# Attention and MoE on one core: batch 0 multiplies each score group with v at once, zero-padded shared block, half of batch 1 in split fp16

## The chip, the cores and the metric

One NeuronCore of a Trainium2 chip runs the kernel. The metric is the device time of one execution in microseconds (us), as the median of several executions. Each program runs alone on its core; there is no communication. TensorE (PE) multiplies into PSUM, ScalarE (ACT) and VectorE (DVE) work on the results, and SyncE (SP) issues nearly all transfers, in the order of its own instruction stream.

## The reference, cut to what matters

```python
# q, k, v: [4 batches, 12 heads, 448, 64] float32; cap = 30
scores = (q @ k.T) / sqrt(64)
scores = cap * tanh(scores / cap)
attn = softmax(scores, axis=-1)            # exp, row sum + 1e-9, division
x = (attn @ v) -> reshaped to [1792 tokens, 768]
h = x @ w_in                               # w_in [768, 2048]
g = h / (1 + exp(-1.702 * h))
out = g @ w_out                            # w_out [2048, 768]
# w_in and w_out arrive as float64, read as pairs of 32-bit words
```

## The kernel before, in words

**Units.** The attention is cut into 24 units (`units`): 4 batches of 6 head pairs. Everything is kept transposed, with keys or features on partitions and the 448 queries of a batch along the free dimension. The 448 keys of each of the two heads make three blocks of 128, and a last block of 64; the two last blocks share one tile of 128 partitions (block number 3, head j in half j). A unit has four score groups (`GROUPS`, line 482): blocks 0 and 4, 1 and 5, 2 and 6, then 3 alone. `scores` (484) multiplies a group into a PSUM tile `s`, takes tanh on ACT (tile `t`) and exp on ACT (tile `p`). The row sums `sm` come from a product with ones, the unnormalised result `pa` from a product with v (`attend`, 566, and `col_tiled`, 536).

**Two precisions.** Batches 0 and 1 (`F32_BATCHES = 2`) use float32 matmuls. Batches 2 and 3 split q, k, p and v into a high and a low fp16 part and add products; that needs casts and subtractions on ACT and DVE for each unit. For those batches the exp tiles of a unit are first added up on DVE (`addup`, tile `ta`).

**Shared block.** For block 3 the kernel uses half-height matmuls on the two halves (`COLS`, row slices), in the array tilings 64x64 and 64x32, while the other blocks use 128x64 and 128x32.

**Normalising.** Most units send their sums (`s4`, a copy of `sm` in ring `f`) to DRAM, fetch them spread over 112 partitions (`sd`, `sr`), invert them there, write them back (`rd`) and read them broadcast (`rb`): a trip of four steps of transfers through the one SP queue. The tile `pa` is copied to `pu` so that PSUM comes free. `DIRECT0` names two units of batch 0 whose sums are made at full width and inverted in place. The result goes to `xh` and `xl`, the fp16 parts of x.

**MoE.** Once the x of a batch is ready, `h_unit` (640) makes 16 feature chunks of 18 matmuls each, and `o_unit` (656) 6 output chunks of 48, all in split fp16; tile names `m`, `gh`, `gl`. `decode_w` (408) turns one fetched tile of weights into two fp16 parts with six operations; there are 24 tiles of w_in and 32 of w_out, and they are fetched by `fetch_w` into buffers which lie in the later w_out space, or in the ring `stg`.

**Order.** The main loop at line 742 calls everything in a program order: after each score group a `slot` adds weight decodes (`DECODE0`, `DECODE1`) and, against a time budget, MoE work. Delay lists (`AV_DELAY`, `SUM_DELAY0`, ...) put the steps of `attend` some slots later. Then `Plan.schedule` (199) simulates engines with the rates in `RATE` and lets the first operation that can start go first, by program order on a tie; it fixes the order on each engine and the buffer of each ring that an operation gets. A ring hands out its buffers in program order of the requests: the request at the head must be served first (line 212). Which engine runs a cast is fixed by `CAST_ON_ACT`, `G_ON_ACT`, `HI_ON_ACT`. On the chip, each engine follows that order and waits on semaphores.

**Start.** The value `cap` is fetched by a GpSimd DMA (line 315); its reciprocal, scaled, is the scale of the first tanh. Sixteen small matmuls on zeros run meanwhile.

Of the kernel before, what the change touches and what calls it, by code (L numbers as in the profile page):

```python
# [30 lines left out]
CAST_ON_ACT = ((), (0, 1), (0, 1, 2, 3), (0, 1, 2, 3))  # L31
G_ON_ACT, HI_ON_ACT = 18, 12
# [10 lines left out]
DMA_ISSUE, DMA_LAG, DMA_BW = 0.38, 2.1, 0.36  # L43
# [44 lines left out]
class Op:  # L88
    __slots__ = ("n", "eng", "us", "emit", "bufs", "left", "users", "ready", "turn", "mb", "start", "end", "tag", "prio")


class Plan:
    def __init__(self, tc):
        self.tc, self.nc = tc, tc.nc
        self.ops = []
        self.rings = []
        self.shift = 0
        self.after = []
# [5 lines left out]
    def ring(self, tiles):  # L104
        r = {"tiles": tiles, "free": [(0.0, i) for i in range(len(tiles))], "queue": []}
        self.rings.append(r)
        return r
# [7 lines left out]
    def op(self, eng, us, emit, writes, reads, turn=None, mb=0.0, tag=""):  # L115
        o = Op()
        o.n, o.eng, o.us, o.emit, o.turn, o.mb, o.tag = len(self.ops), eng, us, emit, turn, mb, tag
        o.prio = o.n + self.shift
# [24 lines left out]

    def act(self, out, in_, func, scale=1.0, bias=0.0):
        n = math.prod(out.shape[1:])
        kind = ("act", "act_ptr", "act_ptr2")[isinstance(scale, Ref) + isinstance(bias, Ref)]
        def emit():
            nc = self.nc
            if func == AF.Copy:
                nc.scalar.activation(real(out), real(in_), func, scale=scale, bias=bias)  # L150
            elif isinstance(bias, Ref):
                nc.scalar.activation(real(out), real(in_), func, scale=real(scale), bias=real(bias))  # L152
            else:
                nc.scalar.activation(real(out), real(in_), func, scale=real(scale))  # L154
        self.op("ACT", RATE[kind][0] + n * RATE[kind][1], emit, [out], [in_, scale, bias])

    def dve(self, name, out, ins, kind="dve", n=None, accum_out=None, **kw):

        f = RATE[kind]
# [5 lines left out]
        self.op("DVE", f[0] + n * f[1] + (0.08 if accum_out is not None else 0.0), emit, w, list(ins.values()))  # L165
# [7 lines left out]
    def scaled(self, out, in_, f):  # L173
        def emit():
            self.nc.vector.tensor_scalar_mul(real(out), real(in_), f)
        n = math.prod(out.shape[1:])
        self.op("DVE", RATE["dve2"][0] + n * RATE["dve2"][1], emit, [out], [in_])

    def copy(self, out, in_):
        def emit():  # L180
            self.nc.vector.tensor_copy(real(out), real(in_))
        n = math.prod(out.shape[1:])
        self.op("DVE", RATE["dve2"][0] + n * RATE["dve2"][1], emit, [out], [in_])

    def mm(self, us, turn, parts):
# [4 lines left out]
        self.op("PE", us, emit, [p[0] for p in parts], [y for p in parts for y in p[1:3]], turn=turn)  # L190

    def dma(self, pairs, mb):
# [3 lines left out]
        self.op("SP", DMA_ISSUE * len(pairs), emit, [p[0] for p in pairs], [p[1] for p in pairs], mb=mb)  # L196


    def schedule(self):
        free = {"PE": 0.0, "ACT": 0.0, "DVE": 0.0, "SP": 0.0}  # L200
        cand = {e: [o for o in self.ops if o.eng == e and not o.left] for e in free}
        turn, pipe = None, 0.0
        order = []
        while len(order) < len(self.ops):
            best = None
            for e, c in cand.items():
                for o in c:
                    t = max(o.ready, free[e])
# [4 lines left out]
                    if t < math.inf:  # L213
                        o.start = t
                        k = (max(t, free[e]), o.prio)
                        if best is None or k < best[0]:
                            best = (k, e, o)
                    else:
                        o.start = t
            assert best is not None, "no step can go on"  # L220
            (t, _), e, _ = best
            o = min((o for o in cand[e] if o.start <= t), key=lambda o: o.prio)
            cand[e].remove(o)
            for b in o.bufs:
                if b.slot is None:
                    b.ring["queue"].pop(0)
                    b.slot = b.ring["free"].pop(0)[1]
            us = o.us
            if e == "PE":
                us += PE_TURN * (o.turn != turn)  # L230
                turn = o.turn
            free[e] = t + us
# [6 lines left out]
            o.start, o.end = t, t + us  # L239
            order.append(o)  # L240
            for u in o.users:
                u.left -= 1
                u.ready = max(u.ready, t + us if u.eng == e and e != "SP" else done + HANDOFF)
                if not u.left:
                    cand[u.eng].append(u)
# [7 lines left out]
        return order  # L253
# [18 lines left out]
def fast_path(ctx, tc, flag, q, k, qx, kx, v, cap, w_in, w_out, out):  # L272
# [9 lines left out]
    NC = 7  # L282
# [21 lines left out]
    ones16 = sb.tile([P, 32], F16, name="ones16")  # L304
    nc.vector.memset(ones16, 1.0)
    ones32 = sb.tile([P, D], F32, name="ones32")
    nc.vector.memset(ones32, 1.0)
# [4 lines left out]
    for _ in range(16):  # L312
        nc.tensor.matmul(ps_m["tiles"][0][:32, :128], ones16, wz, start=True, stop=True)
    capt = sb.tile([P, 1], F32, name="capt")
    nc.gpsimd.dma_start(capt, cap.to_broadcast([P, 1]))
    lnb = sb.tile([P, 1], F32, name="lnb")
    nc.vector.memset(lnb, math.log(64.0))
# [7 lines left out]
    capt, lnb, ones16, ones32 = (plan.fixed(t) for t in (capt, lnb, ones16, ones32))  # L325
# [27 lines left out]
    NW, NA = 2 * W0 * 2, 2 * S  # L353
    early_w = plan.ring([t[:, i * NW:(i + 1) * NW].bitcast(I32).rearrange("p (n t) -> p n t", t=2) for i in range(3) for t in wo_t])
    early = [t[:, 10 * DM + i * NA:10 * DM + (i + 1) * NA].bitcast(F32) for i in range(5) for t in wo_t]
    early_kq = plan.ring(early[:6])
    early_v = plan.ring([t.rearrange("p (c d) -> p c d", d=D) for t in early[6:9]])
# [50 lines left out]
    def decode_w():  # L408
# [16 lines left out]
        if m == 0 and z < G_ON_ACT:  # L425
            plan.scaled(Hf, Hf, 2.0**-112)
        else:
            plan.act(Hf, Hf, AF.Copy, scale=2.0**-112)
        plan.stt(L, H, 3, L, ALU.logical_shift_left, ALU.bitwise_or)
        if m == 1:  # L430
            plan.after = early_bufs["w"] if r < 8 else early_bufs["a"] if r >= 10 else []
        if m == 0 and z < HI_ON_ACT:
            plan.scaled(hi, Lf, WS)
        else:
            plan.act(hi, Lf, AF.Copy, scale=WS)
# [8 lines left out]
    def load_qk(b, p, split):  # L444
# [10 lines left out]
        plan.act(kk, kd, AF.Copy, scale=QS)  # L455
# [4 lines left out]
        plan.act(qh, qd, AF.Copy, scale=QS)  # L460
# [23 lines left out]
    def scores(kt, qt, split, pt, act_cast, addup):  # L484
        qsplit = len(qt) == 2
        for g, cols in enumerate(GROUPS):
# [24 lines left out]
            if split:  # L511
# [6 lines left out]
                if g in act_cast:  # L518
                    plan.act(pb[:, 0, :nn], t[:, :nn], AF.Copy)
                else:  # L520
                    plan.copy(pb[:, 0, :nn], t[:, :nn])
# [12 lines left out]
            yield  # L534

    def col_tiled(o, pt, weights, prods, us):

        for i in range(4):
            parts = []
            for w, (a, bb) in enumerate(prods):  # L540
                for j in range(2):
                    c, rs = COLS[j][i]
                    lhs = ones32[rs] if weights is None else weights[a][rs, c]
                    parts.append((o[j * D:(j + 1) * D, :S], lhs, pt[c][bb][rs], i == 0 and w == 0, i == 3 and w == len(prods) - 1))
            plan.mm(us * len(prods), "64x64" if i == 3 else "128x64", parts)

    def attend_direct(pt, vt, xh, xl):
        sm, pa = plan.turn(ps_sm), plan.turn(ps_pa)
        col_tiled(sm, pt, None, [(0, 0)], 4 * FULL)
        s4 = plan.turn(f_r)  # L550
        plan.act(s4, sm[:, :S], AF.Copy, bias=1e-9)
        col_tiled(pa, pt, vt, [(0, 0)], 4 * FULL)

        def invert():
            plan.dve("tensor_reduce", new_rmin(), dict(in_=s4), n=S, op=ALU.min, axis=AX.X)

        def final():
            r = plan.turn(f_r)
            plan.dve("reciprocal", r, dict(in_=s4), kind="recip")
            plan.tt(r, pa[:, :S], r, ALU.mult)  # L560
            plan.act(xh, r, AF.Copy, scale=XS * VS)
            plan.stt(xl, r, XS * VS, xh, ALU.mult, ALU.subtract)

        return invert, final

    def attend(pt, vt, split, xh, xl, direct=False):
        if direct:
# [408 lines left out]
```

## Time and profile before

| | us |
|---|---|
| median of 3 runs | 661.16 (660.21 to 661.57) |
| the profiled execution's own time | 663.54 |
| span of the profiled execution | 661.4 |
| PE busy in the span | 638.3 (97%) |
| ACT busy | 389.2 (59%) |
| DVE busy | 371.8 (56%) |

A row of a busy table gives the share of the span, but the stages differ: the slices and the windows show them. An interval on a line of the timeline is start, then duration; a bracket behind it is how long the engine had been idle and what it waited for. "x8" counts instructions merged on the line; a float32 matmul appears as two. The unit 0 of the text is the first head pair of batch 0, and unit 6 the first of batch 1.

### The profile page before, as it was taken

Reading aid. Unit: us, or ns where it says so; the run is one execution under the profiler, and the core shown is the slowest. Engines: PE = TensorE matmul, PEld = TensorE weight load, DVE = VectorE, ACT = ScalarE, POOL = GpSimd, SP = SyncE. Lnnn points to the kernel's source line nnn. Section 1 sums busy time; section 2 is a strip of 40 time slices with the busy share of each in tenths; the row PEclk is TensorE's granted clock in tenths of the full one; section 3 lists DMA queues with packets and bytes.
Section 4 is the critical chain, followed back from the end, with each engine's and each line's share of the span. In section 5 each row is a group of like instructions: output and inputs, shape, how many; then the busy total and the mean of one; then the engine's idle time right before and its main releaser. Section 6 shows DMA issues by size and latency. Waiting matters only on the chain.

```text
span 661.4 us, 9003 instructions
## 1 busy us (share of the span) xinstructions
PE 638.3 (97%) x3474; PEld 288.5 (44%) x3474; DVE 371.8 (56%) x746; ACT 389.2 (59%) x557; POOL 0.9 (0%) x5
## 2 busy tenths in 40 slices
PE   6977999999999999999999999999999999999996
PEld 2222224433434445444444544544444455555553
DVE  4998898777765125767864545676764213332000
ACT  4866986878776546867975666787866203331000
POOL 0000000000000000000000000000000000000000
PEclk9988999999999999999999999999999999999999
DMA  8975512555556223022123322110010110000000
GB/s 288 381 270 140 171 46 57 141 152 162 152 174 201 80 62 98 15 85 71 29 71 99 91 65 85 50 49 16 16 42 16 30 42 14 1 1 15 15 29 31
DMA packets 38465, 58.70 MB, mean 89 GB/s; under 512 B 16056, under 2 KB 28176, under 8 KB 38416
## 3 DMA queue, kind: packets, MB, share of 16 engines
q1 hardware_dynamic: 38384, 58.06, 28.7%
q8 instruction: 29, 0.48, 0.3%
q14 instruction: 20, 0.16, 0.1%
q0 software_dynamic: 32, 0.00, 0.0%
HBM read 52.35 MB, written 5.70 MB: 88 GB/s over the span
## 4 chain that ended last, share of the span: by engine, by line
PE 89%; DMA 4%; ACT 3%; DVE 2%; issue 1%; SPq 0%; ACTq 0%; DVEq 0%; POOLq 0%
PE m L189 65%; PE s L189 10%; PE pa L189 9%; PE sm L189 4%; DMA sr<-sd 1%; ACT t L154 1%; DMA capt<-in_cap_dram 1%; ACT p L152 1%; DMA f<-rd 1%; DVE wo_l L163 1%; DVE wi_l L163 0%; DVE wo_h L163 0%; DMA rd<-rr 0%; DMA sd<-f 0%; SPq L195 0%
## 5 line engine op out<-in xcount | busy, mean ns | idle before, releaser
L189 PE MATMUL m<-xh,wi_h 128*128 128x448 f16 x384 | 135.8, 354 | 0.0
L189 PE MATMUL m<-xl,wi_h 128*128 128x448 f16 x384 | 135.6, 353 | 0.0
L189 PE MATMUL m<-xh,wi_l 128*128 128x448 f16 x384 | 135.6, 353 | 0.0
L189 PE MATMUL m<-gh,wo_h 128*128 128x448 f16 x384 | 135.5, 353 | 0.0
L189 PE MATMUL m<-gh,wo_l 128*128 128x448 f16 x384 | 135.4, 352 | 0.0
L189 PE MATMUL m<-gl,wo_h 128*128 128x448 f16 x384 | 135.3, 352 | 0.0
L154 ACT ACTIVATE t<-s,tsc 128x896 f32<-128x896 f32 x96 | 87.0, 909 | 39.1 <-PE s L189 38.9
L189 PEld LDWEIGHTS <-wi_h 128*128 128x128 f16 x768 | 73.3, 98 | 79.5 <-issue 12.5
L189 PEld LDWEIGHTS <-wo_h 128*128 128x128 f16 x768 | 73.7, 98 | 76.1 <-issue 9.2
L154 ACT ACTIVATE f<-m 128x448 f32<-128x448 f32 x64 | 34.8, 544 | 63.0 <-PE m L189 62.6
L163 DVE SCALAR_TENSOR_TENSOR f<-f,m 128x448 f32<-128x448 f32 x64 | 39.6, 619 | 49.3 <-ACT f L154 49.0
L150 ACT ACTIVATE f<-m 128x448 f32<-128x448 f32 x24 | 13.0, 540 | 87.1 <-PE m L189 79.0
L163 DVE TENSOR_TENSOR ta<-ta,t 128x896 f32<-128x896 f32 (+1 forms) x48 | 41.1, 856 | 31.0 <-ACT t L152 30.7
L189 PE MATMUL s<-qh,kk 128*128 128x448 f16 (+2 forms) x192 | 54.0, 469 | 1.4 <-ACT t L154 1.4
L163 DVE SCALAR_TENSOR_TENSOR gl<-f,gh 128x448 f16<-128x448 f32 x64 | 39.8, 622 | 26.6 <-ACT gh L150 26.5
L152 ACT ACTIVATE p<-t,lnb,capt 128x896 f32<-128x896 f32 (+1 forms) x48 | 49.4, 1038 | 7.1 <-PE pa L189 6.0
L189 PEld LDWEIGHTS <-wi_l 128*128 128x128 f16 x384 | 37.6, 98 | 35.2 <-issue 0.2
L189 PEld LDWEIGHTS <-wo_l 128*128 128x128 f16 x384 | 37.6, 98 | 35.1
L150 ACT ACTIVATE gh<-f 128x448 f16<-128x448 f32 x64 | 36.4, 568 | 14.0 <-DVE f L163 14.0
L189 PE MATMUL s<-wo_l,wo_h 64*128 64x448 f32 (+1 forms) x96 | 28.6, 694 | 11.4 <-ACT t L154 10.0
L163 DVE SCALAR_TENSOR_TENSOR stg<-stg 128x384 int32<-128x384 int32 x64 | 35.0, 558 | 4.2 <-ACT stg L150 3.2
L152 ACT ACTIVATE t<-t,lnb,capt 128x896 f32<-128x896 f32 (+1 forms) x36 | 36.2, 1007 | 1.0
(93 smaller groups left out, 625.0 us busy)
## 6 DMA issues: line engine op xcount, KB each, us to landing
stg<-in_moe_w_out_dram SPq DMA_DIRECT2D x32, 384.0 KB
wo_h<-in_moe_w_in_dram SPq DMA_DIRECT2D x12, 512.0 KB
wo_l<-in_moe_w_in_dram SPq DMA_DIRECT2D x12, 512.0 KB
out_dram<-f SPq DMA_DIRECT2D x24, 224.0 KB
stg<-in_kx_dram SPq DMA_DIRECT2D x12, 448.0 KB
stg<-in_qx_dram SPq DMA_DIRECT2D x12, 448.0 KB
f<-rd SPq DMA_DIRECT2D x44, 112.0 KB
vd<-in_v_dram SPq DMA_DIRECT2D x12, 224.0 KB
```

Of the source, the lines that this page charges most:

```text
L150: nc.scalar.activation(real(out), real(in_), func, scale=scale, bias=bias)
L152: nc.scalar.activation(real(out), real(in_), func, scale=real(scale), bias=real(bias))
L154: nc.scalar.activation(real(out), real(in_), func, scale=real(scale))
L163: getattr(self.nc.vector, name)(out=real(out), **{k: real(x) for k, x in ins.items()}, **kw, **a)
L189: self.nc.tensor.matmul(real(o), real(w), real(x), start=a, stop=z)
```

## The change

The change touches the order in which batch 0 is worked, the layout of the shared block, the start, and the planner.

- **v at once.** For float32 units, `attend_step` follows each score group with its share of `pa`, and with `sm` after groups 1 and 3 (each group for direct units). `sm` and `pa` are claimed at a unit's first group.
- **Zero padding.** v has 8 blocks: block 3 is stored twice, with the other head's half zeroed; `ones32` and `ones16` have three versions likewise. All of `pa` runs in tiling 128x64 and all of `sm` in 128x32 (128x64 for direct units).
- **Start.** `cap` is the first DMA of SP; an activation on a small tile (`warm`) loads the table of ACT early.
- **Split.** `F32_UNITS = 9`: units 9 to 11, the second half of batch 1, go in split fp16, with their row sums by four fp16 steps (no `addup`).
- **Planner.** Casts and PSUM copies may go to ACT or DVE, chosen in the simulation (`ways`, with `DVE_SHY`); the delay lists are gone; the ring `f` of six becomes `f` (3, any order), `rb` (2) and `pu` (2); the ring `p` goes from 6 to 5; `DMA_ISSUE` and `DMA_LAG` grow. Fewer weight tiles are decoded before batch 1 (`PAUSE`), more within it (`DECODE1`).

```diff
-DECODE1 = (1, 2)
-PAUSE = (2, 3)
-AV_DELAY = (0, 1, 2)
-SUM_DELAY0 = (1, 1, 2, 2, 3, 4)
-SUM_DELAY = (1, 2, 3, 3, 4, 5)
-DIRECT_DELAY = (5, 0)
-F32_BATCHES = 2
+DECODE1 = (2, 2)
+PAUSE = (2, 1)
+F32_UNITS = 9
-CAST_ON_ACT = ((), (0, 1), (0, 1, 2, 3), (0, 1, 2, 3))
-G_ON_ACT, HI_ON_ACT = 18, 12
+PE_STAY = 0
-DMA_ISSUE, DMA_LAG, DMA_BW = 0.38, 2.1, 0.36
+DMA_ISSUE, DMA_LAG, DMA_BW = 0.5, 2.6, 0.36
+ACT_FROM = 4.0
+DVE_SHY = 2.0
...
+    def scaled(self, out, in_, f=None, on="AV", psum=False, bias=None):
...
+        ways = {}
+        if "V" in on:
+            ways["DVE"] = (self.cost("dve" if psum else "dve2", n), on_dve)
+        if "A" in on:
+            ways["ACT"] = (self.cost("act", n), on_act)
+        self.op(ways, [out], [in_])
...
-                            t = max(t, r["free"][0][0]) if r["queue"][0] is b and r["free"] else math.inf
+                            t = max(t, r["free"][0][0]) if r["free"] and (r["any"] or r["queue"][0] is b) else math.inf
+                    p = o.prio + (PE_STAY if e == "PE" and o.turn != turn else 0)
+                    k = (t, p, o.ways[e][0])
...
-    NC = 7
+    NC = 8
...
+    capt = sb.tile([P, 1], F32, name="capt")
+    nc.sync.dma_start(capt, cap.to_broadcast([P, 1]))
+    lnb = sb.tile([P, 1], F32, name="lnb")
+    nc.vector.memset(lnb, math.log(64.0))
+
+    warm = sb.tile([P, 1], F32, name="warm")
+    nc.scalar.activation(warm, lnb, AF.Tanh)
+
+    ones32 = [sb.tile([P, D], F32, name=f"ones32_{i}") for i in range(3)]
+    ones16 = [sb.tile([P, 32], F16, name=f"ones16_{i}") for i in range(3)]
...
-    capt = sb.tile([P, 1], F32, name="capt")
-    nc.gpsimd.dma_start(capt, cap.to_broadcast([P, 1]))
...
-    p_t = [sb.tile([P, 2, 2, S], F16, name=f"p{i}") for i in range(6)]
+    p_t = [sb.tile([P, 2, 2, S], F16, name=f"p{i}") for i in range(5)]
-    f_r = ring([P, S], F32, "f", 6)
+    f_r = ring([P, S], F32, "f", 3)
+    f_r["any"] = True
+    rb_r = ring([P, S], F32, "rb", 2)
+    pu_r = ring([P, S], F32, "pu", 2)
...
-    COLS = (
-        [(0, slice(0, P)), (1, slice(0, P)), (2, slice(0, P)), (3, slice(0, D))],
-        [(4, slice(0, P)), (5, slice(0, P)), (6, slice(0, P)), (3, slice(D, P))],
-    )
+    COLS = (((0, 0), (1, 1), (2, 2), (3, 3)), ((4, 4), (5, 5), (6, 6), (3, 7)))
...
+    def row_sums(sm, pt, split, steps):
+        for i in steps:
+            parts = []
+            for w in range(2):
+                for j in range(2):
+                    k = i if split else 2 * i + w
+                    c, g = COLS[j][k][0], 2 * j + w
+                    one = 2 if k < 3 else j
+                    lhs, rhs = (ones16[one], pt[c][w]) if split else (ones32[one][:, :32], pt[c][0])
+                    parts.append((sm[32 * g:32 * g + 32, :S], lhs, rhs, i == 0, i == (3 if split else 1)))
+            plan.mm(FULL if split else 4 * FULL, "128x32", parts)
+
+    def attend_step(pt, vt, g, direct):
+        if g == 0:
+            pt["sm"], pt["pa"] = plan.turn(ps_sm), plan.turn(ps_pa)
+        if direct:
+            col_tiled(pt["sm"], pt, None, [(0, 0)], 4 * FULL, [g])
+        elif g % 2:
+            row_sums(pt["sm"], pt, False, [g // 2])
+        col_tiled(pt["pa"], pt, vt, [(0, 0)], 4 * FULL, [g])
...
-        split = b >= F32_BATCHES
+        split = u >= F32_UNITS
+        direct = b == 0 and p in DIRECT0
         tb = BUDGET[b]
-        for c, _ in enumerate(scores(kt, qt, split, pt, CAST_ON_ACT[b], split)):
-            if c == 1 and b:
+        x = xs[b, p] = [plan.turn(r) for r in x_r[p]]
+        for g in scores(kt, qt, split, pt, b >= 2):
+            if not split:
+                attend_step(pt, vt, g, direct)
+            if g == 1 and b:
                 prepare(u + 1)
-            slot(tb, DECODE1[p // 3] if b else DECODE0[c])
+            slot(tb, DECODE1[p // 3] if b else DECODE0[g])
...
+    last = _np.zeros((B, NP, 2, 128, D), vv.dtype)
+    last[:, :, 0, :64], last[:, :, 1, 64:] = vv[:, :, 0, 384:], vv[:, :, 1, 384:]
```

## Rows read from the trace of the kernel before

**Rows 1.** Windows: length, busy us and (count) of PE, PEld, DVE, ACT, POOL; granted clock, DMA share, GB/s.

```profile
10.00:40.00 30.00, 27.54 (x116) 6.49 (x116) 28.53 (x54) 25.31 (x28) 0.00 (x0) 1.00 1.02 383
40.00:94.00 54.00, 45.50 (x210) 13.14 (x209) 48.25 (x88) 42.05 (x60) 0.00 (x0) 0.94 0.50 142
94.00:120.00 26.00, 26.00 (x134) 11.58 (x134) 22.61 (x53) 15.73 (x29) 0.00 (x0) 1.00 0.21 61
120.00:200.00 80.00, 80.00 (x409) 32.21 (x406) 60.63 (x166) 64.26 (x107) 0.00 (x0) 1.00 0.55 154
200.00:260.00 60.00, 60.00 (x314) 25.83 (x313) 23.46 (x40) 35.63 (x48) 0.00 (x0) 1.00 0.34 105
```

**Rows 2.** Timeline, the first 10 us: cap, the first scores, the first tanh.

```profile
1.20 0.42 SPq L195 DMA_DIRECT2D wo_l<-in_q_dram  x1
1.24 0.66 POOL L315 DMA_DIRECT2D capt<-in_cap_dram  x1 [0.79 <-POOLq L950]
4.19 3.36 PE L189 MATMUL s<-wo_l,wo_h 64*128 64x448 f32 x8 [1.22 <-DMA wo_l<-in_q_dram]
...
8.14 0.16 DVE L319 RECIPROCAL rc<-capt 128x1 f32<-128x1 f32 x1 [7.00 <-DMA capt<-in_cap_dram]
...
9.87 1.01 ACT L154 ACTIVATE t<-s,tsc 128x896 f32<-128x896 f32 x1
```

**Rows 3.** Timeline, 27 to 78 us: sums, their copies, the transfers of units 0 and 2.

```profile
27.87 0.64 SPq L195 DMA_DIRECT2D sd<-f  x1
...
30.85 1.82 PE L189 MATMUL sm<-p,ones 128*32 128x448 f32 x8
...
44.38 0.53 ACT L150 ACTIVATE f<-sm 128x448 f32<-128x448 f32 x1
45.82 3.22 PE L189 MATMUL sm<-p,ones 128*32 128x448 f32 x16
...
56.01 0.62 DVE L163 TENSOR_TENSOR f<-f,f 128x448 f32<-128x448 f32 x1 [1.11 <-ACT p L152]
...
63.96 0.52 SPq L195 DMA_DIRECT2D sd<-f  x1
...
77.78 0.61 DVE L163 TENSOR_TENSOR f<-f,f 128x448 f32<-128x448 f32 x1
```

**Rows 4.** Groups by line in 0 to 94 us: busy us, mean ns | idle before.

```profile
L189 PE MATMUL s<-qh,kk 64*128 64x448 f32 x12 | 3.1, 588 | 1.4 <-ACT t L154 1.4
L189 PE MATMUL m<-xh,wi_h 128*128 128x448 f16 x7 | 2.7, 387 | 0.0
```

**Rows 5.** Chain that ended last, in order of time: TensorE's runs in batches 0, 1 and 2.

```profile
17.21 0.90 PE pa L189 x4
...
138.18 2.50 PE sm L189 x16
140.68 3.31 PE pa L189 x16
143.98 0.95 PE s L189 x4
...
265.44 2.51 PE pa L189 x24
267.95 0.86 PE s L189 x4
...
272.22 0.76 PE s L189 x4
...
276.38 0.50 PE s L189 x4
```

**Rows 6.** Groups by line over the whole span, shapes apart.

```profile
L163 DVE TENSOR_TENSOR p<-t,p 128x896 f16<-128x896 f32 x24 | 26.0, 1084 | 0.0
L150 ACT ACTIVATE p<-t 128x896 f16<-128x896 f32 x24 | 22.8, 950 | 0.8
L163 DVE SCALAR_TENSOR_TENSOR wo_l<-wo_l 128x512 int32<-128x512 int32 x24 | 16.7, 694 | 0.7
```

More of the change, by code (lines that the diff above doesn't have):

```diff
@@ L88 @@
 class Op:
[L89 removed]
+    __slots__ = ("eng", "ways", "emit", "bufs", "left", "users", "ready", "turn", "mb", "start", "end", "prio")
 class Plan:
@@ L104, in ring @@
     def ring(self, tiles):
-        r = {"tiles": tiles, "free": [(0.0, i) for i in range(len(tiles))], "queue": []}
-        self.rings.append(r)
-        return r
+        return {"tiles": tiles, "free": [(0.0, i) for i in range(len(tiles))], "queue": [], "any": False}
     def turn(self, ring):
@@ L195, in emit @@
                 self.nc.sync.dma_start(real(o), real(i))
-        self.op("SP", DMA_ISSUE * len(pairs), emit, [p[0] for p in pairs], [p[1] for p in pairs], mb=mb)
+        self.op({"SP": (DMA_ISSUE * len(pairs), emit)}, [p[0] for p in pairs], [p[1] for p in pairs], mb=mb)
     def schedule(self):
-        free = {"PE": 0.0, "ACT": 0.0, "DVE": 0.0, "SP": 0.0}
-        cand = {e: [o for o in self.ops if o.eng == e and not o.left] for e in free}
+        free = {"PE": 0.0, "ACT": ACT_FROM, "DVE": ACT_FROM, "SP": 0.0}
+        cand = {e: [o for o in self.ops if e in o.ways and not o.left] for e in free}
         turn, pipe = None, 0.0
@@ L207, in schedule @@
                 for o in c:
-                    t = max(o.ready, free[e])
+                    t = max(o.ready + (DVE_SHY if e == "DVE" and len(o.ways) > 1 else 0.0), free[e])
                     for b in o.bufs:
@@ L211, in schedule @@
                             r = b.ring
-                            t = max(t, r["free"][0][0]) if r["queue"][0] is b and r["free"] else math.inf
[L213 to L223, printed above, removed]
+                            t = max(t, r["free"][0][0]) if r["free"] and (r["any"] or r["queue"][0] is b) else math.inf
+                    p = o.prio + (PE_STAY if e == "PE" and o.turn != turn else 0)
+                    k = (t, p, o.ways[e][0])
+                    if best is None or k < best[0]:
+                        best = (k, e, o)
+            assert best is not None and best[0][0] < math.inf, "no step can go on"
+            (t, _, us), e, o = best
+            for w in o.ways:
+                cand[w].remove(o)
+            o.eng, o.emit = e, o.ways[e][1]
             for b in o.bufs:
                 if b.slot is None:
-                    b.ring["queue"].pop(0)
+                    b.ring["queue"].remove(b)
                     b.slot = b.ring["free"].pop(0)[1]
-            us = o.us
             if e == "PE":
@@ L231, in schedule @@
                 turn = o.turn
+            o.start, o.end = t, t + us
             free[e] = t + us
@@ new lines, in attend @@
+    def attend(pt, vt, split, xh, xl):
+        if not split:
+            sm, pa = pt["sm"], pt["pa"]
+        else:
+            sm, pa = plan.turn(ps_sm), plan.turn(ps_pa)
+            if "sum" in pt:
+                h = S // 2
+                plan.mm(4 * FULL / 2, "128x32", [
+                    (sm[32 * g:32 * g + 32, :h], ones32[2][:, :32], pt["sum"][:, g // 2, (g % 2) * h:(g % 2 + 1) * h], True, True) for g in range(4)
+                ])
+            else:
+                row_sums(sm, pt, True, range(4))
+            col_tiled(pa, pt, vt, [(0, 0), (0, 1), (1, 0)], FULL)
@@ L623, in back @@
-        def back():
-            box["rd"] = plan.turn(rd_r)
-            plan.dma([(box["rd"].rearrange("j (p m) -> p j m", m=RW), box["rr"])], 0.02)
-        def broadcast():
-            rb = box["rb"] = plan.turn(f_r)
-            plan.dma([(rb[j * D:(j + 1) * D], box["rd"][j:j + 1].to_broadcast([D, S])) for j in range(2)], 0.3)
-        def final():
-            r = box["rb"]
-            plan.tt(r, pa[:, :S], r, ALU.mult)
-            sc = XS if split else XS * VS
-            plan.act(xh, r, AF.Copy, scale=sc)
-            plan.stt(xl, r, sc, xh, ALU.mult, ALU.subtract)
@@ L640, in h_unit @@
+        plan.dve("reciprocal", rr, dict(in_=rs), kind="recip")
+        rd = plan.turn(rd_r)
+        plan.dma([(rd.rearrange("j (p m) -> p j m", m=RW), rr)], 0.02)
+        rb = plan.turn(rb_r)
+        plan.dma([(rb[j * D:(j + 1) * D], rd[j:j + 1].to_broadcast([D, S])) for j in range(2)], 0.3)
+        plan.tt(rb, pa[:, :S], rb, ALU.mult)
+        sc = XS if split else XS * VS
+        plan.scaled(xh, rb, sc)
+        plan.stt(xl, rb, sc, xh, ALU.mult, ALU.subtract)
     def h_unit(b, fc):
```

264 lines of the change are left out of this document (98 added, 166 removed).

## The prediction

> **What bounds the kernel now.** I read the page's slices first, then the windows by stage, the waits of TensorE, the chain, and the timeline of the first 100 us. From 94 us on TensorE is full: 26.00 of 26.00 us, 80.00 of 80.00, 60.00 of 60.00 [rows 1], so there only less TensorE work shortens the time. Before 94 us it isn't. It is called busy for 45.50 of 54 us between 40 and 94 [rows 1], but that counts matmuls which stand in the array while it waits, and some of it ran at a lowered clock (0.94 granted on average). The waits name ACT's tanh as what TensorE waits for most in this stage. The reader should see two things in the timeline. First, the start: the scores of the first two groups begin at 4.19, and the first tanh only at 9.87, because cap, fetched by GpSimd at 1.24, is read by DVE at 8.14 [rows 2], 6.9 us later, and the table load of ACT stands behind it. Second, lumps: unit 1's sums end near 32.7, their copy out of PSUM runs at 44.38, and unit 2's sums follow at 45.82 in one lump [rows 3]. The copy was planned so late because ring f serves in program order, and the request for unit 0's broadcast stood ahead of it. While ACT works the scores, TensorE has no v product to do; while TensorE does the lump, ACT finds no exp buffer free.
>
> **The start.** cap is SP's first transfer, so k and q come about one issue later, 0.42 us [rows 2]: the scores start near 4.6. They ran at half rate there, 3.36 us for eight matmuls against 0.95 for four [rows 5], so the first group ends near 6.3. cap on SP has no row; a trip's four steps take 13.8 us in all (63.96 to 77.78) [rows 3], so one small transfer is about 3.5 us, above 2 and at worst the 6.9 of the old path. At 3.5 it lands near 4.2, and with the reciprocal and the scale (9.87 − 8.14, less the table load that is now hidden) it stands by 5 us. The scores end last: tanh at 6.4, not 9.87, 3.4 us gained. Late next is ACT itself, at some 2 us a group.
>
> The Trainium skill, "DMA: Bandwidth & Descriptors", section "Specifications", gives the GpSimd path about 1 us to the first byte and SP's 0.6 us. By that alone the move is worth 0.4 us, since then the 6.9 us would be crowding and not the path. No row here separates the two; the sum uses the rows, and the page's way is a rival below.
>
> **Batch 0.** Three floors for the point at which TensorE becomes full (94 before):
> - TensorE. Unit by unit in the new order: four score groups at 0.95, four v groups at 0.90, two sum steps at 0.95 (padding makes both steps four products side by side, where 2.50 us stood for three runs) = 9.3 us; direct units take 3.31 for sums instead of 1.9 [rows 5]. Six units: 4 × 9.3 + 2 × 10.7 = 58.6. Before 94 it had also done unit 6's four score groups (12 float32 matmuls and the last four), half its sums, and 20 MoE matmuls of 0.19 (7 + 7 + 6) [rows 4]: 3.8 + 0.95 + 3.8 = 8.5, taken as the same after. With 4.6 of start and at least 1.5 for the half rate (3.36 − 1.9): 73.
> - ACT and DVE together. They were busy 28.53 + 25.31 + 48.25 + 42.05 = 144.1 us in 10 to 94 [rows 1]. By the program order 22 weight tiles stood before batch 1, and after only 16 stand before batch 0's last x. One tile is six operations of 0.53 on average (28.53/54) [rows 1], up to 0.69 [rows 6], so six tiles fewer are 19 us. Unit 6's tanh and exp, some 7.5 us, needn't come first. That leaves 117.6. In 10 to 40 the two were busy 53.84 of 60 us, 89.7%, the most that any window shows; at that rate 117.6 take 65.5 us, from about 8: 74. Free choice of engine is what lets them reach it.
> - The trips. Ring pu has two buffers, so unit 2's copy waits for unit 0's product, and ps_pa with it. A trip took 28.1 us under the weight stream (27.87 to 56.01) and 13.8 later [rows 3]. Unit 0's sums end near 16, unit 2's v product near 35; the trip ends at 30 or at 44: 0 to 9 us of wait. SP issues in order, so a trip also waits behind fetches whose buffers are undecoded; that queue is unchanged, with v's transfers an eighth longer.
>
> I put 6 us for the third on top of 74 and take 80: **14 us gained**, the start included. Bounds: 20.5 (no wait) and 3.4 (only the start). What the lumps cost goes; late next are ACT and DVE.
>
> **Units 9 to 11 in fp16.** Before, a unit took 3.8 of scores, 2.50 of sums, 3.31 of v: 9.6. In batch 2 scores take 0.86 + 2 × 0.76 + 0.50 = 2.88 [rows 5]; four fp16 sum steps stream the columns of one float32 step, 0.95 (0.76 without any entry); v takes 2.51 less one change of tiling. That change costs 0.145: 0.90 for one v group and 3.31 for four with two entries give 0.755 a group. So 6.2, and **10.2 us gained** in three (9.5 to 11.7 with the shorter MoE re-entries). No wait hides it: TensorE is full there.
>
> **Padding in batches 2 and 3.** One entry less in 12 units, 0.11 each: **1.3** (0 to 1.7). Bigger v tiles add an eighth to two short DVE operations a unit, beside TensorE.
>
> **Units 6 to 8.** Sums fall by 0.6, v in four runs costs 0.3 more, and up to five more returns to MoE cost 0.1 each: **0**, ±0.7 a unit.
>
> **What batch 1 must now carry.** From 94 to 260, DVE was busy 106.7 and ACT 115.6 us [rows 1], 222 of 332. To this come the 19 us of postponed decode, and for each split unit five copies of 0.95 and five subtractions of 1.08 of full length [rows 6] and four shorter ones, 12.4 in all: 37. That is 278, in a window of 166 − 10 = 156 us: 89%, again the most the two have shown. Behind a late decode stands the MoE output, and behind a late cast the next scores; TensorE has the other to fall back on. I take **3 us lost** (0 if casts move to the faster engine, 12 if not). Planner rates, deeper DMA estimates and smaller rings have no row of their own; they act through these three floors.
>
> **Sum.** 14 + 10.2 + 1.3 + 0 − 3 = 22.5. The profiled execution took 663.54 (span 661.4 and 2.1 around), so 641.0 by it; it stands 2.4 above the median of 661.16, and to the median the sum is 638.7. What can be told from no change here is about 0.2%, 1.3 us.
>
> **Rivals.**
> - *The trips go on pacing batch 0.* If unit 0's trip takes its 28.1 us and the others follow in pairs, only the start is gained: 3.4 + 10.2 + 1.3 − 3 = 11.9, 649.3. For it: SP's order is unchanged where DMA share is 1.02. Against: sums no longer wait for the broadcast's buffer. Chance 0.20.
> - *Everything fits.* 20.5 + 10.2 + 1.3, no loss: 629.2. Against: 89% of two engines with no wait. Chance 0.12.
> - *Batch 1 starves TensorE (slower).* If ACT and DVE reach only the 74% of 94 to 120 (38.3 of 52) [rows 1], 278 us need 188 and not 156: 32 lost against 25.5 gained, 667.7. It decides from 76.6%: 278/(2 × 181.5). In 94 to 200 they ran at 77%. Against: there they were waiting for TensorE, so this was no limit of theirs. Chance 0.13, of which 0.04 within 0.2%.
> - *cap stays late.* If the 6.9 us are crowding, cap lands near 7.7, tanh starts at 8.2 without the table load, 1.7 gained and not 3.4: 640.4. This is the page's way. Chance 0.05.
>
> **How the numbers follow.** My forecast has 0.50, with 632 to 646 as its own range. The range 629 to 655 holds it, the late cap, the pacing with some loss in batch 1, and the best case at its edge; left out are most of starvation and a little on the low side. Faster: 0.50 + 0.20 + 0.12 + 0.05 = 0.87; same 0.04; slower 0.09.
>
> **What would show it.** In the profile after: first tanh near 6.4; v products of four between score groups, and no lump of sums and v in batch 0; every sums run in tiling 128x32; TensorE full from about 80; three split units' runs of about 2.9, 0.95 and 2.4 late in batch 1; ACT and DVE near 90% to the end of the weight decode, with short waits of TensorE there. Wrong: TensorE waiting in batch 0 for copies behind pu, or more than 12 us of waits between 80 and 240, or a decode of w_out that the MoE output waits for.

## The result, and the profile after

The changed kernel takes **641.27 us** (median of 4 runs, 639.26 to 642.25) against 661.25 us (median of 4) for the kernel before. The ratio is 0.9697, with a 95% interval of 0.967 to 0.9723. The profiled execution took 641.68 us with a span of 639.4, so 22.0 us of span are gone. The prediction was 638.7 in a range of 629 to 655: sign and range hold, and the forecast was 2.6 us too low. Underneath, the terms are less tidy than the sum.

First the page's slices of the kernel after, where the span stands in 40 pieces of 16 us. TensorE is at 7 in the first two slices and, but for one 8 and the last slice, at 9 from the third on; in the second, 16 to 32 us, the granted clock is down to 8 tenths.

```profile
PE   7798999999999999999999999999999999999996
PEclk9899999999999999999999999999999999999999
```

Next the windows by stage, which answer to [rows 1]; columns as there.

```profile
10.00:40.00 30.00, 26.31 (x122) 6.06 (x124) 26.77 (x52) 29.50 (x42) 0.00 (x0) 0.94 1.01 381
40.00:94.00 54.00, 49.84 (x254) 17.25 (x251) 47.42 (x89) 44.92 (x64) 0.00 (x0) 1.00 0.45 123
94.00:120.00 26.00, 26.00 (x136) 10.31 (x135) 21.57 (x55) 21.14 (x36) 0.00 (x0) 1.00 0.39 117
120.00:200.00 80.00, 80.00 (x447) 34.77 (x446) 67.74 (x165) 67.72 (x112) 0.00 (x0) 1.00 0.59 168
200.00:260.00 60.00, 60.00 (x366) 28.34 (x364) 42.42 (x69) 44.06 (x60) 0.00 (x0) 1.00 0.42 128
```

The reader should see three things. ACT is busy for 29.50 of 30 us in the first window, where DVE was the busier one before. From 94 us TensorE is still full, so what is saved there is work and not waiting. And batch 1 now carries much more on the two other engines (135.46 of 160 us in 120 to 200, 85%) without a gap on TensorE.

The start, from the timeline, against [rows 2]:

```profile
0.75 0.39 SPq L303 DMA_DIRECT2D capt<-in_cap_dram  x1
3.83 0.17 DVE L324 RECIPROCAL rc<-capt 128x1 f32<-128x1 f32 x1 [1.93 <-DMA capt<-in_cap_dram]
6.98 1.01 ACT L147 ACTIVATE t<-s,tsc 128x896 f32<-128x896 f32 x1 [4.74 <-PE s L190]
```

The first tanh is at 6.98 and no longer waits for `cap`, but for the scores. Then batch 0, against [rows 3]: the copies of the v products out of PSUM (`pu<-pa`), the v products that follow them, and the matmul at which TensorE becomes full.

```profile
23.95 1.76 PE L190 MATMUL pa<-p,wo_l 128*64 128x448 f32 x4 [2.82 <-ACT p L147]
...
49.90 0.62 DVE L155 TENSOR_TENSOR rb<-pu,rb 128x448 f32<-128x448 f32 x1
50.77 0.62 DVE L176 COPY pu<-pa 128x448 f32<-128x448 f32 x1
51.44 3.23 PE L190 MATMUL pa<-p,wo_l 128*64 128x448 f32 x16
...
59.38 0.53 ACT L171 ACTIVATE pu<-pa 128x448 f32<-128x448 f32 x1
59.95 1.72 PE L190 MATMUL pa<-p,wo_h 128*64 128x448 f32 x8 [1.93 <-ACT pu L171]
...
85.70 0.35 PE L190 MATMUL m<-xh,wi_h 128*128 128x448 f16 x1 [0.72 <-DVE f L155]
```

Units 0 to 2 go as planned, v beside the scores. Unit 2's copy at 50.77 stands right behind unit 0's product, which frees the ring `pu`, and so unit 3 has its sixteen v matmuls in one lump at 51.44. TensorE is full from 85.70 on. In the kernel before its last wait ends at 89.51, and batch 0's last v product is done at 93.7, the point that the sums here use:

```profile
89.51 0.96 PE L189 MATMUL sm<-p,ones 128*32 128x448 f32 x8 [0.49 <-ACT f L150]
90.40 3.38 PE L189 MATMUL pa<-p,wo_h 128*64 128x448 f32 x16
93.71 0.36 PE L189 MATMUL m<-xh,wi_h 128*128 128x448 f16 x1
```

Batches 1 and 2 in the chain, against [rows 5]: the second sum step and a v group of unit 6, in float32, then a score group, two runs of row sums and a v product of split units.

```profile
101.69 0.89 PE sm L190 x8
102.58 0.90 PE pa L190 x4
...
155.19 0.76 PE s L190 x4
...
170.55 0.49 PE sm L190 x8
...
178.27 0.30 PE sm L190 x4
...
229.16 2.39 PE pa L190 x24
```

**Where the 22.0 us come from.** Up to these two points, 8.0 us. By then TensorE had also done more work ahead: 36 MoE matmuls (12 of each of the three products, one of which is below) against 18 (of the 20 up to 94 in the prediction, two start behind 93.7), and three score groups and one v group of unit 6 (3.75 us) against four score groups and half the sums (4.75). That is 18 × 0.19 − 1.0 = 2.4 us more, so batch 0 gave 10.4 us and all that follows 11.6.

```profile
L190 PE MATMUL m<-xl,wi_h 128*128 128x448 f16 x12 | 4.2, 352 | 0.0
```

### The profile page after: what moved, and what is told of

It is laid out like the page before. It is cut to its first block, busy times and chain, and to the rows that moved or that the text cites. A ratio compares the mean times of both kernels' runs of the same rounds, so it can differ in the third digit from the quotient of the medians.

```text
span 639.4 us, 9126 instructions
## 1 busy us (share of the span) xinstructions
PE 622.3 (97%) x3498; PEld 286.7 (45%) x3498; DVE 385.0 (60%) x766; ACT 400.6 (63%) x585; POOL 0.2 (0%) x4
## 4 chain that ended last, share of the span: by engine, by line
PE 90%; DMA 4%; ACT 3%; DVE 1%; issue 0%; SPq 0%; ACTq 0%; DVEq 0%
PE m L190 69%; PE pa L190 9%; PE s L190 9%; PE sm L190 3%; DMA rb<-rd 1%; DMA sr<-sd 1%; DMA wo_l<-in_moe_w_in_dram 1%; DMA sd<-f 1%; ACT t L147 1%; ACT p L147 0%; DMA rd<-rr 0%; ACT wi_h L171 0%; ACT wo_l L171 0%; ACT wo_h L171 0%; SPq L196 0%
## 5 line engine op out<-in xcount | busy, mean ns | idle before, releaser
L147 ACT ACTIVATE f<-m 128x448 f32<-128x448 f32 x64 | 34.6, 543 | 57.5 <-PE m L190 55.8
L171 ACT ACTIVATE f<-m 128x448 f32<-128x448 f32 x22 | 11.9, 541 | 86.2 <-PE m L190 78.0
L147 ACT ACTIVATE t<-t,lnb,capt 128x896 f32<-128x896 f32 (+1 forms) x48 | 48.8, 1016 | 1.2
L190 PE MATMUL s<-qh,kk 128*128 128x448 f16 (+3 forms) x168 | 49.0, 420 | 0.4 <-ACT t L147 0.4
L155 DVE TENSOR_TENSOR p<-t,p 128x896 f16<-128x896 f32 (+1 forms) x48 | 45.1, 939 | 1.1 <-ACT p L171 0.9
L171 ACT ACTIVATE p<-t 128x896 f16<-128x896 f32 (+1 forms) x47 | 38.6, 821 | 0.4
L147 ACT ACTIVATE p<-t,lnb,capt 128x896 f32<-128x896 f32 (+1 forms) x36 | 37.4, 1038 | 0.8
```

The costliest lines, as they stand in the source:

```text
L147: self.nc.scalar.activation(real(out), real(in_), func, scale=real(scale), **b)
L171: self.nc.scalar.activation(real(out), real(in_), AF.Copy, scale=1.0 if f is None else f, **b)
L190: self.nc.tensor.matmul(real(o), real(w), real(x), start=a, stop=z)
```

## Experiments

Each ran beside the kernel before, on the same chip. "Ratio" is to the kernel before; the changed kernel has 0.9697. A difference between two ratios is turned into us with 661.25; one of less than about 2 us can't be told from none by the two intervals.

**A third buffer for pu (e1).** Does batch 0 wait for the trips?

```diff
-    pu_r = ring([P, S], F32, "pu", 2)
+    pu_r = ring([P, S], F32, "pu", 3)
```

> The changed kernel with three pu buffers instead of two. Theory (the trips pace batch 0 through pu: unit 2's and unit 3's copies run at 50.77 and 59.38, right behind the products of units 0 and 1): the copies come up to 8 us earlier, TensorE is full some 3 to 7 us sooner, 634 to 638 us. Rival (ACT, busy over 98% between 10 and 50 us, is the bound): the copies move, the time does not: 640 to 642 us.

640.05 us, ratio 0.9674 (0.9649 to 0.9698). The copies do come early, and with them the lump goes:

```profile
43.77 0.53 ACT L171 ACTIVATE pu<-pa 128x448 f32<-128x448 f32 x1
...
53.84 0.53 ACT L171 ACTIVATE pu<-pa 128x448 f32<-128x448 f32 x1
```

TensorE's wait for `pu` falls from 1.9 to 0.5 us, but the time by 1.5 us, which the intervals don't show. The wait was real and cost little: while v is held, TensorE has other work, and its waits for ACT's tanh grow from 1.6 to 2.7 us.

**No split (e2).**

```diff
-F32_UNITS = 9
+F32_UNITS = 12
```

> The changed kernel with all of batch 1 in float32 again (F32_UNITS = 12). Theory (each converted unit saves 3.4 us of a full TensorE): 10 us slower, 650 to 652 us. Rival (the split's casts cost waits in batch 1 that eat part of it): only 3 to 7 us slower, 644 to 648 us.

648.96 us, ratio 0.9798 (0.9779 to 0.9817). The split is worth 0.0101 × 661.25 = 6.7 us, and not 10.2.

**v after all four score groups (e3).** The change's first item undone, the planner left free.

```diff
         for g in scores(kt, qt, split, pt, b >= 2):
-            if not split:
-                attend_step(pt, vt, g, direct)
...
+        if not split:
+            for g in range(4):
+                attend_step(pt, vt, g, direct)
```

> The changed kernel with the v products and sums of a float32 unit called behind its last score group instead of behind each one. Theory (v at once is what keeps TensorE fed while ACT works the scores): batch 0 gets its lumps back, 4 to 8 us slower, 645 to 650 us. Rival (what helped was the copies no longer queueing behind the broadcast in ring f; the order of calls matters little to a planner that starts what is ready): 640 to 643 us.

639.50 us, ratio 0.966 (0.9642 to 0.9679). Calling v behind each group gave nothing; the point estimate is 2.4 us on the other side, at the edge of what can be told. The v products still run beside the scores here, in fours from 24 to 43 us, so this run undoes the order of the calls and not what it was meant to bring about. The order in which the code records a unit decides priorities only; what becomes ready starts early anyhow, as long as its PSUM tile and its copy's buffer are to be had. TensorE is full from 84.24 here, 1.5 us sooner; why is not settled.

**Half-height matmuls again (e4).** Block 3 without zero padding, both in the sums and in v.

```diff
-                    lhs = ones32[2 if i < 3 else j] if weights is None else weights[a][:, cv]
+                    rs = slice(0, P) if i < 3 else slice(j * D, (j + 1) * D)
+                    lhs = ones32[2][rs] if weights is None else weights[a][rs, cv]
...
-            plan.mm(FULL if split else 4 * FULL, "128x32", parts)
+            plan.mm(FULL if split else 4 * FULL, "64x32" if i == (3 if split else 1) else "128x32", parts)
```

> The changed kernel with the shared key block in half-height matmuls again, on the same padded v. Theory: 0.6 to 0.85 us per float32 sums step that falls into two runs, for three units of batch 1, and 0.11 us per change of tiling in 15 split units: 3.5 to 4.5 us slower, 645 to 646 us; batch 0 hides its own part. Rival (the sums steps hide beside other work and the changes of tiling cost nothing): within 1 us, 640 to 642 us.

647.37 us, ratio 0.9782 (0.9762 to 0.9803): padding is worth 5.6 us. The chain shows where. The first step of a unit's sums is the full-height one here; the second one, with block 3, is not:

```profile
90.55 0.89 PE sm L190 x8
...
103.55 1.75 PE sm L190 x8
```

Eight matmul instructions of one height (four products) run side by side in 0.89 us, and four of full and four of half height take 1.75. The Trainium skill, "TensorEngine Tiling (Array Packing)", section "Key Properties", says that changing the tiling mode drains TensorE; that agrees with the sign here, but it names no price, and 0.86 us a step is one run more, not a short drain.

**The weights' casts on VectorE (e5).** Takes from ACT what stands ahead of the exps.

```diff
+VZ = 16
-        plan.scaled(Hf, Hf, 2.0**-112)
+        plan.scaled(Hf, Hf, 2.0**-112, on="V" if m == 0 and z < VZ else "AV")
```

(and the same for the cast to `hi`)

> The changed kernel with both casts of the first 16 weight tiles held on DVE (0.43 us each there, 0.68 on ACT, which does 17 of them between 10 and 50 us). Theory (with a third pu buffer changing nothing, ACT is what bounds batch 0: it is busy 98% there): 11.6 us of ACT work leave the stretch and TensorE is full 3 to 6 us sooner, 635 to 638 us. Rival (DVE, busy 89% there, takes 7.3 us more and becomes the bound): 640 to 645 us.

643.40 us, ratio 0.9721 (0.9703 to 0.9739), 1.6 us more, less than can be told. The windows show the exchange: the first is full on TensorE, and the gap comes later.

```profile
10.00:40.00 30.00, 30.00 (x160) 7.21 (x159) 28.52 (x53) 27.39 (x33) 0.00 (x0) 1.00 1.05 395
40.00:94.00 54.00, 44.48 (x215) 15.20 (x212) 49.83 (x92) 35.27 (x51) 0.00 (x0) 0.94 0.42 124
```

The waits of TensorE (total us, times, longest) name it:

```profile
PE pa L191 <- DVE pu L177: 7.8, 1, 7.8
```

ACT's exps come sooner, so TensorE runs ahead into the two buffers of `pu` and waits there 7.8 us. Now DVE is the one without a pause: its decode steps are the chain from 20 to 53 us, and in 44 to 56 it is busy for 11.07 of 12 us and ACT for 2.72. The gap moved from 24 us to the stretch before 55, and the time didn't fall, as the rival had it.

**Decode placed as before (e6).**

```diff
-DECODE1 = (2, 2)
-PAUSE = (2, 1)
+DECODE1 = (1, 2)
+PAUSE = (2, 3)
```

> The changed kernel with the weight decodes called as before (DECODE1 = (1, 2), PAUSE = (2, 3)): four more tiles ahead of batch 1. Theory (the postponed decode is one part of what shortened batch 0: 13 us of ACT and DVE work over two engines): TensorE full some 3 to 6 us later, 644 to 647 us. Rival (the planner starts what is ready, the calls' place matters little): 640 to 642 us.

641.21 us, ratio 0.9681 (0.9662 to 0.9701): no difference that can be told. Where the tiles stand in the program does not say when they are decoded.

**The kernel before with a ring of its own for the broadcasts (e7).**

```diff
-    f_r = ring([P, S], F32, "f", 6)
+    f_r = ring([P, S], F32, "f", 4)
+    rb_r = ring([P, S], F32, "rb", 2)
...
-    rb = box["rb"] = plan.turn(f_r)
+    rb = box["rb"] = plan.turn(rb_r)
```

> The kernel before with its ring f of six cut into f (4) and a ring of its own for the broadcasts (2), nothing else. Theory (the copies of sm and pa came 11.7 us late because the broadcast's request stood ahead of them in ring f): batch 0 loses part of its lumps, 3 to 8 us faster than before, 653 to 658 us. Rival (the trips pace the units anyway): 660 to 662 us.

652.95 us, ratio 0.9862 (0.9841 to 0.9883): **9.1 us** with the same six buffers and none of the other edits. The copies behind unit 0's broadcast come without delay (44.38 in [rows 3] is 31.39 here), and the window 10 to 40 is full. The timeline, then the windows:

```profile
31.39 0.54 ACT L150 ACTIVATE f<-sm 128x448 f32<-128x448 f32 x1 [1.42 <-PE sm L189]
```

TensorE has 30.00 of 30 us and 48.88 of 54, against 27.54 and 45.50 in [rows 1], and the granted clock of the second window is 1.00 where it was 0.94:

```profile
10.00:40.00 30.00, 30.00 (x136) 6.64 (x134) 28.52 (x54) 24.99 (x29) 0.00 (x0) 1.00 1.03 385
40.00:94.00 54.00, 48.88 (x237) 14.82 (x234) 46.90 (x85) 43.56 (x59) 0.00 (x0) 1.00 0.47 140
```

**cap on GpSimd's queue again (e8).** At the same early place, with the table loaded early.

```diff
-    nc.sync.dma_start(capt, cap.to_broadcast([P, 1]))
+    nc.gpsimd.dma_start(capt, cap.to_broadcast([P, 1]))
```

> The changed kernel with cap fetched by GpSimd again, from the same early place, ACT's table load still early. Theory (the path costs 6.9 us from issue to reading, the rows of before): cap is read near 7.5 us, the first tanh runs near 8 and not 6.98, 0 to 1.5 us slower, 641 to 643 us. Rival (the page's 0.4 us between the two paths; the 6.9 us were the crowd of transfers ahead of it): cap is read near 4.3 us and nothing moves, 641 us.

641.46 us, ratio 0.9687 (0.9668 to 0.9706): no difference.

```profile
1.24 0.66 POOL L303 DMA_DIRECT2D capt<-in_cap_dram  x1 [0.78 <-POOLq L917]
...
5.92 0.16 DVE L324 RECIPROCAL rc<-capt 128x1 f32<-128x1 f32 x1 [4.00 <-DMA capt<-in_cap_dram]
6.37 1.01 ACT L147 ACTIVATE t<-s,tsc 128x896 f32<-128x896 f32 x1 [4.12 <-DVE tsc L328]
```

From issue to reading it took 4.7 us, against 3.1 on SP's queue (0.75 to 3.83), and 6.9 in the kernel before. The first tanh comes at 6.37 and waits for the scale made from `cap`; that is sooner than the 6.98 of the changed kernel, where it waits for scores that start at 5.08 and not, as here, at 3.93. The Trainium skill, "DMA: Bandwidth & Descriptors", section "Specifications", has 1 against 0.6 us to the first byte for the two paths; here they are 1.6 us apart, from issue to use and not to the first byte, four times that difference, and the end doesn't depend on either.

**One ring in program order again (e9).** f, rb and pu of the changed kernel share seven buffers.

```diff
-    f_r = ring([P, S], F32, "f", 3)
-    f_r["any"] = True
-    rb_r = ring([P, S], F32, "rb", 2)
-    pu_r = ring([P, S], F32, "pu", 2)
+    f_r = rb_r = pu_r = ring([P, S], F32, "f", 7)
```

> The changed kernel with its seven f, rb and pu buffers in one ring that serves in program order, as ring f did before. Theory (head of line in ring f made the lumps; cutting it took 8.9 us off the kernel before): the copies of sm and pa come late again and batch 0 loses 5 to 9 us, 646 to 650 us. Rival (v at once and the free choice of engine have made up for it, or one buffer more is enough): 640 to 643 us.

656.46 us, ratio 0.9911 (0.9892 to 0.993): 14.2 us of the gain gone, with as many buffers. The copy of unit 3's v product, which ends near 63.8, runs only at 70.10, and TensorE's next v product waits for it. The gaps go on into batch 1 (39.18 of 40 and 37.53 of 40 us busy), where the changed kernel has none. The timeline:

```profile
70.10 0.53 ACT L171 ACTIVATE f<-pa 128x448 f32<-128x448 f32 x1
...
70.68 0.97 PE L190 MATMUL pa<-p,wo_h 128*64 128x448 f32 x4 [1.25 <-ACT f L171]
```

And the windows:

```profile
120.00:160.00 40.00, 39.18 (x206) 15.19 (x205) 31.50 (x84) 29.05 (x48) 0.00 (x0) 1.00 0.47 140
160.00:200.00 40.00, 37.53 (x218) 18.13 (x217) 34.70 (x82) 31.92 (x52) 0.00 (x0) 1.00 0.55 162
```

**The whole start undone (e10).** cap on GpSimd's queue at its old place, and no early table load.

```diff
-    capt = sb.tile([P, 1], F32, name="capt")
-    nc.sync.dma_start(capt, cap.to_broadcast([P, 1]))
...
-    warm = sb.tile([P, 1], F32, name="warm")
-    nc.scalar.activation(warm, lnb, AF.Tanh)
...
+    capt = sb.tile([P, 1], F32, name="capt")
+    nc.gpsimd.dma_start(capt, cap.to_broadcast([P, 1]))
     rc = sb.tile([P, 1], F32, name="rc")
```

> The changed kernel with the start of before: cap fetched by GpSimd behind the warm-up matmuls' code, ACT's table loaded before the first tanh. Theory (the start's 2.9 us between the two first tanhs pass to the end): first tanh 8 to 10 us, 642.5 to 645 us. Rival (batch 0 waits for other things later, which swallow it): 640 to 642 us.

642.48 us, ratio 0.9694 (0.9677 to 0.9711): no difference, though the first tanh stands at 9.04, 2.06 us later.

```profile
9.04 1.01 ACT L147 ACTIVATE t<-s,tsc 128x896 f32<-128x896 f32 x1
...
87.69 0.35 PE L190 MATMUL m<-xh,wi_h 128*128 128x448 f16 x1 [0.74 <-DVE f L155]
```

In this profile TensorE is full from 87.69 and not 85.70, so batch 0 does keep the 2 us; they don't show in the time, and the interval (±1.1 us for this kernel, ±1.7 for the changed one) can hold them. The start is worth 0 to 2 us, not 3.4.

**All of batch 1 in split fp16 (e11).** One step further in the change's own direction.

```diff
-F32_UNITS = 9
+F32_UNITS = 6
```

> The changed kernel with all of batch 1 in split fp16 (F32_UNITS = 6). Theory (a converted unit saves 2.2 to 2.9 us of a full TensorE, and ACT and DVE, together at 80% between 94 and 260 us, can carry 37 us more): 6 to 8 us faster, 633 to 636 us. Rival (at 91% of both engines the casts come late and TensorE waits): 638 us or slower.

649.66 us, ratio 0.979 (0.9765 to 0.9814): three more units in fp16 cost 6 us instead of giving some 7. A window, and then TensorE's waits between 94 and 200 us, show the starvation that the prediction feared for three units:

```profile
120.00:160.00 40.00, 34.00 (x198) 15.63 (x196) 37.79 (x91) 33.88 (x57) 0.00 (x0) 0.96 0.56 169
```

Total us, times, longest:

```profile
PE m L190 <- DVE f L155: 4.8, 5, 1.6
```

In 120 to 160 the two engines are busy for 71.67 of 80 us (89.6%), DVE alone for 94%, and TensorE has gaps of 6.0 us, and of 2.3 in 160 to 200. The largest wait is of the MoE matmuls for an operation of VectorE that writes an f, five times, at most 1.6 us.

**Together (e12).** v after the scores, three buffers for pu and all of batch 1 in split fp16 (the edits of e3, e1 and e11).

> All of batch 1 in split fp16, three pu buffers, and v products called behind a unit's last score group (in batch 0, the only float32 batch left). Theory (each helped or did no harm by itself): 631 to 635 us, below the changed kernel and below the one with F32_UNITS = 6 alone by 0 to 3 us. Rival (a full ACT and DVE in batch 1 decide): as that one.

652.85 us, ratio 0.9851 (0.9829 to 0.9873), 4 us above e11. So what helps a little with three split units does not add up with six; the two small edits can't be read as gains of their own. TensorE's gaps in 120 to 200 are 10.2 us here and 8.3 in e11; why, no run shows. No kernel tried beats the changed one clearly: e3 comes nearest, at the edge of the intervals.

## Why the prediction was right, and where its terms were not

**Batch 0: 14 predicted, 10.4 found.** Of its three floors the prediction let the two other engines decide, and their rate came near the forecast. That they are the bound fits e5, where work taken off ACT filled DVE and gained nothing; no run isolates it, and the chain from 34 to 59 us runs through unit 1's trip. The term that was mis-sized is the work: "six tiles fewer are 19 us", and 117.6 us left. The windows of the changed kernel, up to its full point:

```profile
8.00:40.00 32.00, 28.31 (x128) 6.73 (x128) 28.56 (x55) 31.47 (x44) 0.00 (x0) 0.95 1.01 381
40.00:60.00 20.00, 16.93 (x90) 4.68 (x86) 14.77 (x33) 16.14 (x22) 0.00 (x0) 1.00 0.69 178
60.00:85.70 25.70, 24.62 (x121) 8.97 (x121) 24.61 (x40) 20.52 (x31) 0.00 (x0) 1.00 0.39 113
```

ACT and DVE together did 136.1 us there, 87.6% of 77.7. At the predicted 89.7% that work takes 75.9 us from 8: 83.9, and TensorE is full at 85.7. Only two tiles fewer were decoded by then, not six: the last step of a tile stands 9 + 9 times in the groups of 0 to 85.7, and stood 10 + 10 times in those of the kernel before up to 93.7.

```profile
L155 DVE SCALAR_TENSOR_TENSOR wi_l<-wo_h,wi_h 128x512 f16<-128x512 f32 x9 | 6.2, 694 | 1.6 <-ACT wi_h L171 1.6
L155 DVE SCALAR_TENSOR_TENSOR wi_l<-wo_l,wi_h 128x512 f16<-128x512 f32 x9 | 6.2, 689 | 0.1
```

```profile
L163 DVE SCALAR_TENSOR_TENSOR wi_l<-wo_l,wi_h 128x512 f16<-128x512 f32 x10 | 6.9, 688 | 0.2
L163 DVE SCALAR_TENSOR_TENSOR wi_l<-wo_h,wi_h 128x512 f16<-128x512 f32 x10 | 6.9, 685 | 1.2 <-ACT wi_h L150 1.0
```

Up to the start of batch 1 the program itself has 22 and 18; the prediction counted 16, up to batch 0's last x. The planner starts a tile when its data and an engine are there; e6 shows that its place in the program doesn't matter. The free choice of engine also cost work: up to the two points 27 casts of the weight tiles ran on ACT, and 14 before, at 0.68 us each where DVE takes 0.43. That it is what lets the two engines reach 89.7% no run shows, and e7, with the fixed choice, has 53.51 of 60 us (89.2%) in 10 to 40. The 6 us put on top for the trips were wrong too: the trips pace the copies (50.77 right behind 49.90), and still the third buffer gives 1.5 us, less than can be told (e1). Two errors of opposite sign left 80 against 85.7.

**What removed the lumps.** The prediction read the cause from [rows 3] as the order of ring `f`, and that is shown: its own ring for the broadcasts gives 9.1 us in the kernel before (e7), and one ring in the kernel after takes 14.2 (e9). It let the calls of v behind each group share the credit; by e3 they aren't needed, since the v products run beside the scores without them. The gap between 9.1 and 14.2 isn't taken apart: e9 also gives back the free order of `f`, and it carries the split units.

**The start: 3.4 predicted, 0 to 2 found** (e8, e10). The steps were right, tanh at 6.98 against a forecast of 6.4, and cap read 3.1 us after its issue against 3.5. But the next ACT work is decoding: from 10 to 20 us ACT is busy for 9.97 of 10, and its casts and two copies stand ahead of the exp that TensorE waits for at 23.95. The start's rival, a cap that stays late, forecast 640.4 and lies nearest to the result, but not by its mechanism: cap did come early. Behind that wait the granted clock was lower for a while:

```profile
10.00:20.00 10.00, 9.14 (x44) 1.99 (x44) 8.53 (x15) 9.97 (x15) 0.00 (x0) 1.00 1.04 399
20.00:30.00 10.00, 7.18 (x30) 1.54 (x28) 8.65 (x18) 9.93 (x15) 0.00 (x0) 0.83 1.04 402
24.00:26.00 2.00, 2.00 (x6) 0.54 (x8) 1.73 (x4) 1.97 (x3) 0.00 (x0) 0.50 1.03 400
```

0.83 is a mean: part of those 10 us ran at 1.2 GHz (0.50 in 24 to 26) and the rest at 2.4. The two runs after that wait, v at 23.95 and scores at 25.64, take 1.76 and 1.66 us in the chain instead of 0.90 and 0.95. In e1's profile the same wait of 2.8 us left the clock at 1.00, so this price isn't paid each time.

**The split: 10.2 predicted, 6.7 found** (e2). A split unit takes 6.4 us in the chain and not 6.2: 0.76 × 3 + 0.50 of scores, 1.1 to 1.2 of row sums in three or four runs where 0.95 was forecast, and 2.39 to 2.63 of v. The float32 unit beside it was mis-sized: 9.6 was its length before, but in e2 it takes 3.75 of scores, 2 × 0.89 of sums (padding had already taken 0.72 of the 2.50 in [rows 5]) and 4 × 0.90 of v, 9.1 in all. Three units give 8.1. In e2 TensorE is also full 0.7 us sooner, from 85.02, with the same work ahead, which leaves 7.4; the other 0.7 no run places, and the intervals of the two ratios allow it.

**The padding: 1.3 predicted in batches 2 and 3, 5.6 found in all** (e4). The prediction had it in three places and called it only "one entry less" in the last, where it was right: a v product of a split unit takes 2.51 us in e4's chain and 2.39 in the changed kernel's, 1.4 in 12 units. In units 6 to 8 it is 0.86 a unit, 2.6 us, which the prediction took as 0.6 and set off against v in four runs and more returns to MoE. The v products of all split units, units 9 to 11 too, are busy for 1.7 us more in e4. In batch 0 it is 0.7: without padding TensorE is full at 86.42 and not 85.70, with the same work ahead. That is 5.0; 0.6 is left, within the intervals.

**Batch 1: −3 predicted, 0 found.** The rival of starvation was put at 278 us in 156, 89%. The windows show 264.6 us of ACT and DVE in 94 to 260, 80%, and TensorE full throughout, since four of the six "postponed" tiles were decoded in batch 0. The prediction's point that the engines had been waiting for TensorE was right: they ran at 85% in 120 to 200 without a gap, past the 74% of its rival. e11 shows that the mechanism exists, with 89.6% and gaps of 6.0 us in 40. But the share of the two engines doesn't mark where it begins, as two shorter windows show, the first of the changed kernel and the second of e11:

```profile
160.00:180.00 20.00, 20.00 (x123) 9.46 (x122) 17.72 (x38) 18.26 (x28) 0.00 (x0) 1.00 0.59 179
```

```profile
120.00:140.00 20.00, 17.01 (x96) 7.67 (x95) 18.06 (x43) 16.69 (x29) 0.00 (x0) 0.91 0.47 155
```

At 90% TensorE is full in the first, and at 87% it has 3.0 us of gaps in the second. The waits name single operations that came late in e11; why they were late there and not in the changed kernel is not shown.

**The sum.** Ring 9.1, split 6.7 and padding 5.6 make 21.4 against 20.0 measured by the medians; the start, the calls for v, the place of the decode and the size of ring pu are each within 2.4 us of nothing. The 9.1 was measured in the kernel before and the other two in the changed one, so their sum agrees with the total without proving it. The late stages gave 11.6, as much as split and padding have there (6.7 + 5.6 − 0.7). That the forecast came so near is in part luck: 3.6 us too much in batch 0 and 3.5 in the split stand against 3.6 too little for padding behind batch 0 (5.6 − 0.7 − 1.3) and a loss of 3 in batch 1 that didn't come. Open remain the 2.4 us of e3 and e12 against e11. Not tried alone were the free choice of engine, the planner's rates, the smaller ring p, and a faster trip (its transfers on another queue).

## What to carry to other kernels

Look for a request that waits for a transfer at the head of a ring served in order: here it held short copies for 12 us and cost 9 to 14 us in all, and one experiment with a ring of its own prices it. When a floor is made of work that a planner may start at will, count the work that will be ready, not what the program text places there. Trading TensorE time for casts pays until the casts come late: three units gave 6.7 us here, and three more took 6 back. The busy share alone didn't tell where that begins (90% in 20 us without a gap, 87% with one), so try each further step and read TensorE's waits in the stage where it lands.

## What the hardware showed that was not expected

- A sum step of four full-height and four half-height float32 matmuls takes 1.75 us and not 0.89: tiles of two heights didn't run side by side.
- The same four-byte broadcast took 4.7 us from issue to reading on GpSimd's queue in e8, 5.5 in e7 (1.24 to 6.77), 6.1 in e10 (1.24 to 7.31) and 6.9 in the kernel before, all issued at 1.24, and 3.1 on SP's (2.9 to 3.4 in the other runs that have it there). What makes the first four differ is not known.
- A wait of 2.8 us on TensorE was followed by a granted clock of 0.50 in 24 to 26 us, and in e1 the same wait by 1.00. In e5 the wait of 7.8 us was followed by 0.50 in 54 to 58 us and a run of 16 v matmuls of 4.86 us, against 3.23 in the changed kernel.
